# Gated linear attention and a two-layer expert on one core: all wide products in float16 halves, layer two two units behind

## The chip, the cores and the metric

The kernel runs on one core of a Trainium2 chip. The metric is the device time of one execution in microseconds. A core has TensorE (matrix products, from SBUF into PSUM), VectorE, ScalarE and GpSimd (elementwise work), and SyncE, which here issues the transfers. The engines run side by side and wait for one another by semaphores; each works through its own instructions in a fixed order.

## The reference

Two parts, one feeding the other (B=4 sequences, H=8 heads, S=768 steps, D=48 per head; 384 -> 2048 -> 384 in the expert):

```python
f = 1.0 / (1.0 + np.exp(-f_logit))
for t in range(S):
    state = f[:, :, t, :, None] * state + np.einsum('bhd,bhe->bhde', k[:, :, t], v[:, :, t])
    y[:, :, t] = np.einsum('bhd,bhde->bhe', q[:, :, t], state)
x = y.transpose(0, 2, 1, 3).reshape(B * S, H * D)
h = x @ w_in
g = np.where(h >= 1, h, np.where(h <= -1, 0.0, (h + 1) ** 2 / 4))
out = g @ w_out
```

The weights come as float64 and the result is float32.

## The kernel before

The 768 steps are cut into six blocks of 128 (NI = 6). Within a block the attention of a pair of heads is done by products of scores, values and the carried state; a block's 4 x 128 tokens (N = 512 columns) then go through the expert. The expert works in *units*: unit k is block i = k // 16 and 128 of the 2048 hidden channels, j = k % 16. Layer one of a unit is nine matmuls of 128x128 weights by 128x512 values (three thirds of the input, three terms each) into one of two PSUM banks `ph`; layer two is nine more (three thirds of the output, three terms each) that accumulate over the 16 units of a block into the three banks `po`. There are 96 units, and so 1728 of these *wide products*.

The three terms make up for the narrow operands: a value is split into a rounded part and a remainder, and the product is rounded x rounded, rounded x remainder and remainder x rounded. In blocks 0 and 1 all parts are float32r (`mm_in` L356, `mm_out` L390). From block FROM = 2 on, only the rounded x rounded term is float32r; the other two take float16 (`mm_in_16` L363, `mm_out_16` L397). For that, every weight is converted once during block 1: `convert` (L534, L535) makes float16 copies on ScalarE in a staging tile and a transfer (L537) puts them in the place of `w_lo`; each late unit also makes a float16 copy of its rounded activations (`act_16`, L377) and each attention result one of its rounded part (L862).

Between the layers a unit takes five steps: `act_1` (L366, ScalarE) and `act_2` (L369, ScalarE) make the square branch, `act_3` (L374, VectorE) the maximum and minimum, `act_hi` (L380, ScalarE) the rounded part, `act_lo` (L383, VectorE) the remainder. The weights arrive as float64 words: `split_piece` takes the bits apart (L514 ScalarE, L516 VectorE) and splits them into `w_hi` (L520, ScalarE) and `w_lo` (L521, VectorE), one piece for each unit of layer one (384 columns) and twelve pieces of layer two (512 columns), during block 0.

In blocks 0 and 1 layer two runs one unit behind: nine of layer one, nine of layer two. From block 2 on it runs by pairs of units: eighteen of layer one, eighteen of layer two. The attention of the next block is put between. `TURNS` says behind which unit a pair's keys are transposed (L840 on TensorE for block 1, L854 on VectorE after that), and `VISITS` gives four places for each two pairs: scores (`scores_of_two`, L814), states (`states_by_parts`, L1004), the begin of the output (`begin`, L892) and its end (`outputs`, L892 and L923). A place k is behind layer one of unit k, k.5 behind the layer two that follows. A visit borrows a `ph` bank and gives it back when its masks (L826) or sums (L1008) are done. `begin` ends with a small copy (L903, ScalarE) for which the next products of the visit wait. `outputs` rounds the result (L876 and L877, later L860 and L861) and issues moves (L965) that fill the remaining rows of the block's input; the first unit of the block waits for them. `largest` (L871) takes the maximum of the rounded part, which the closing test reads.

Everything is entered into a plan as an operation with an engine, a cost and its dependencies; `Plan.order` plays it through with the table COST and gives each engine its order, the operation with the least room first. `early` on an operation ranks it sooner.

Of the kernel before, what the change touches and what calls it, by code (L numbers as in the profile page):

```python
# [10 lines left out]
F32 = mybir.dt.float32  # L11
# [30 lines left out]
FROM, UP, MOST = 2, 14, 16.0  # L42
SLACK, WITHIN = 2500, 1200
# [15 lines left out]
COST = dict(mm=227, narrow=120, mm16=216, late=690, narrow16=114, scores=1000, scores_half=500, heads=940, thirds=940, half=330, both=940, begin=430, before=880, part=450, states=700, before_half=440, parts=730, parts_last=730, zeros=4860, turn=395, first=160, last=200,  # L59
# [176 lines left out]
def gla_moe(ctx: ExitStack, tc: tile.TileContext, ff, kqd, f0, vv, vad, vbd, wd, fixedd, gates, values, headsd, out):  # L236
# [14 lines left out]
    v_all = const.tile([C, 2 * B * 4 * D], F32, name="v")  # L251
    v = [v_all[:, k * B * 4 * D:(k + 1) * B * 4 * D].rearrange("u (b h e) -> u b h e", b=B, h=4) for k in range(2)]
# [9 lines left out]
    forms, x_hi = {}, tiles(2, [128, NP - 1, N], F32R, "x_hi")  # L262

    def of_form(name, shape, form):
# [5 lines left out]
    def form_of(i):  # L270
        return "late" if i >= FROM else "early"

    def x_at(i):
        return x_hi[i % 2], of_form(f"x{i % 2}", [128, NP - 1, N], form_of(i))

    def y3_at(i):
        return of_form("y3", [R, 2, N], form_of(i))

    def glo_at(k):
        return of_form(f"glo{k % 2}", [128, N], form_of(k // NJ))  # L280

# [9 lines left out]
    w_16 = w_lo.rearrange("p n c -> p (n c)").bitcast(F16).rearrange("p (n k t c) -> p n k t c", n=2 * NW, t=2, c=128)  # L291
# [5 lines left out]
    later = const.tile([128, 2 * B * D], F32, name="later")[:R]  # L297
    ds.append(const.tile([128, 2 * B * D], F32, name="ds")[:R])
# [39 lines left out]
    def w_in_16(t, j, kt):  # L338

        return w_16[:, j // 4 * 3 + kt, j % 4, t]  # L340

    def w_out_16(t, j, e):
        n, c = divmod(j * DM + e * 128, W)
        return w_16[:, NW + n, c // 128, t]

    def of_16(t):

        return t.bitcast(F16)[..., 0:N], t.bitcast(F16)[..., N:]

# [4 lines left out]
    def mm_in(ps, xt, j, c=ALL, to=ALL, a=0, z=9):  # L354
        for n, (kt, high, t) in list(enumerate(TERMS_IN))[a:z]:
            nc.tensor.matmul(ps[:, to], w_in(w_hi if high else w_lo, j, kt), xt[t][:, kt, c], start=(n == 0), stop=(n == 8))  # L356

    def mm_in_16(ps, xt, j, which):
        for n in which:
            for kt in range(3):  # L360
                low, x_16 = of_16(xt[1][:, kt])
                a, b = ((w_in_16(0, j, kt), x_16), (w_in_16(1, j, kt), low), (w_in(w_hi, j, kt), xt[0][:, kt]))[n]
                nc.tensor.matmul(ps, a, b, start=(n == 0 and kt == 0), stop=(n == 2 and kt == 2))  # L363
# [21 lines left out]
    def mm_out(hi, lo, j, es, terms, c=ALL, of=ALL):  # L385
        for e in es:
            for n in terms:
                part, g = ((w_hi, hi), (w_lo, hi), (w_hi, lo))[n]

                nc.tensor.matmul(po[e][:, c], w_out(part, j, e), g[:, of], start=(j == 0 and n == 0 and c.start == 0), stop=(j == NJ - 1 and n == 2))  # L390

    def mm_out_16(hi, lo, j, es, terms):
        low, g_16 = of_16(lo)
        for e in es:
            for n in terms:
                a, b = ((w_out(w_hi, j, e), hi), (w_out_16(0, j, e), g_16), (w_out_16(1, j, e), low))[n]
                nc.tensor.matmul(po[e], a, b, start=(j == 0 and n == 0), stop=(j == NJ - 1 and n == 2))  # L397
# [13 lines left out]
    def copy_out(e, o, up=0):  # L411
        (by_scalar if e == 1 else by_vector)(o, po[e], up)
# [34 lines left out]
    set_ds = add("POOL", 200, lambda: fresh(ds[0][:, 2 * B * D:]))  # L447
# [45 lines left out]
    def split_piece(k):  # L493
# [31 lines left out]
    last_use, again_of = {}, {}  # L525

    passing = []

    def convert(key, n, hi, lo, to):

        m = len(passing)
        past = passing[m - 6:m - 5]
        mem = raw[2 + m % 6 // 2].bitcast(F16)[:, m % 2 * 2 * W:m % 2 * 2 * W + 2 * n].rearrange("p (k t c) -> p k t c", t=2, c=128)
        o = sca(COST["copy"] * n // W, lambda: nc.scalar.activation(mem[:, :, 0], lo.bitcast(F32), AF.Copy, scale=2.0 ** UP), split[key], past, piece[-3:])  # L534
        z = sca(COST["copy"] * n // W, lambda: nc.scalar.copy(mem[:, :, 1], hi.bitcast(F32)), o)  # L535
        z.slack = SLACK
        passing.append(add("SP", "near", lambda: nc.sync.dma_start(to.bitcast(F32), mem.bitcast(F32)), z, last_use[key], kb=n // 2))  # L537
        passing[-1].slack = SLACK
        again_of[key] = passing[-1:]

    def convert_unit(j):

        at = (slice(None), slice(j // 4 * 3, j // 4 * 3 + 3), slice(j % 4 * 128, j % 4 * 128 + 128))
        convert(("unit", j), 384, w_hi[at], w_lo[at], w_16[:, j // 4 * 3:j // 4 * 3 + 3, j % 4])

    def convert_piece(c):

        convert(c, W, w_hi[:, c].rearrange("p (k c) -> p k c", c=128), w_lo[:, c].rearrange("p (k c) -> p k c", c=128), w_16[:, c])
# [6 lines left out]
    def small_piece(c):  # L555

        cuts = 2 if c < 9 else 1
        mem = raw[2 + c % 3]
        loaded = [dma(mem[:, k:k + W // cuts], wd[c, :, k:k + W // cuts], 8 * 128 * W / 1024 / cuts, seen[-6:-4] or passing[-6:])
# [8 lines left out]
    def split_again(c):  # L568
# [17 lines left out]
        nc.scalar.copy(w_hi[:, c], val)  # L586
        nc.vector.tensor_tensor(out=w_lo[:, c], in0=val, in1=w_hi[:, c].bitcast(F32), op=ALU.subtract)
# [91 lines left out]
    def elementwise(n):  # L679
# [14 lines left out]
        if p == NP - 1:  # L694

            cols = slice(0, 2 * N + B) if i else slice(0, N)
            gone = old(n - NP, "sc", "y", "tr", "db")
            c["to"] = []
            for t, m in enumerate(ours):
                o = gates_of[m]  # L700
                d = [o["km"], o["qm"], o["pf"][0]] if i else o["km"]
                o["to"] = [move(kq[NP - 1][z + 16 * SLICE[t]:z + 16 * SLICE[t] + 16, cols], kq[t][r:r + 16, cols], 64 if i else 32, d, set_kq, gone) for r, z in ((48, 0), (112, 64))]
                c["to"].extend(o["to"])
        c["kq"] = c["to"] if p == NP - 1 else [gates_of[m][a] for m in ours for a in ("km", "qm")]
        c["db"] = []
        if i > 0:
# [7 lines left out]
            c["db"].append(sca(B * COST["decay"], decayed, d, state_of[i - 1, p // 2], old(n - 4, "y", "se"), set_ds))  # L714
# [143 lines left out]
    def rounded_16(b, yf, to, y, past, cost=None):  # L858
        hi, low, x_16 = (lambda n=n: to()[n] for n in range(3))
        eh = sca(cost or "round", lambda: nc.scalar.activation(hi(), yf, AF.Copy, scale=2.0 ** UP), y, past)  # L860
        el = vec(cost or "dve", lambda: nc.vector.scalar_tensor_tensor(out=low(), in0=yf, scalar=2.0 ** UP, in1=hi().bitcast(F32), op0=ALU.mult, op1=ALU.subtract), eh)  # L861
        es = sca(cost or "copy", lambda: nc.scalar.activation(x_16(), hi().bitcast(F32), AF.Copy, scale=2.0 ** -UP), eh)  # L862
        banks[b] = [eh, el]
        return [eh, el, es]

    seen_x = {}

    def largest(i, t, *deps):

        at = 1 + NG + 6 * NW + NT * (i - FROM) + t  # L870
# [34 lines left out]
    def outputs(n, unit, alone, joint=False):  # L905
# [36 lines left out]
        def third(t):  # L942
            return [moved.get(i - 1)] if t == NT else [free]
# [567 lines left out]
```

## Time and profile before

| | |
|---|---|
| median of 3 runs | 458.86 us (458.3 to 459.25) |
| profiled execution | 458.67 us |
| its span, first to last instruction | 456.9 us |
| granted TensorE clock, mean | 0.999 |

The profile is of one execution. Busy time is the union of an engine's instructions; PE is TensorE's matmuls, PEld its weight loads, DVE VectorE, ACT ScalarE, POOL GpSimd, SP SyncE. Matmuls overlap in the array: one of 128x512 is shown some 0.38 us long, while the next one starts some 0.22 us after it. So the pace is read from starts, or from a run of many.

### The profile page before, as it was taken

The page shows a single profiled execution, that of the slowest core. Times are in us where ns is not written, and L with a number is a line of the kernel's source. Part 1 is how long each engine was busy: PE and PEld are TensorE (multiplying, and loading weights), DVE is VectorE, ACT ScalarE, POOL GpSimd, SP SyncE. Part 2 cuts the span into 40 slices and gives each one's busy share as a digit, 9 for nine tenths or more (in the row PEclk, how much of TensorE's full clock was granted, in tenths as well). Part 3 has the DMA queues.
Part 4 walks back from the last instruction along what each step waited for, and adds up shares of the span by engine and source line. Part 5 has one row for each costly group of instructions (what it writes and reads, how often), then busy time and mean ns, then how long its engine had stood idle before and what let it go on. Part 6 is the DMA issues. An engine that isn't in the chain of part 4 may idle for free.

```text
span 456.9 us, 11340 instructions
## 1 busy us (share of the span) xinstructions
PE 450.6 (99%) x4540; PEld 305.7 (67%) x4540; DVE 372.7 (82%) x727; ACT 330.8 (72%) x645; POOL 22.1 (5%) x67
## 2 busy tenths in 40 slices
PE   8999999999999999999999999999999999999996
PEld 4888888888888886665665656656655665556563
DVE  7988998989979989988788888966767978877423
ACT  4599999898889986676766766866656674756653
POOL 4200100010000100000100000001000000000000
PEclk9999999999999999999999999999999999999999
DMA  8897767445245356630320330320201534853001
GB/s 288 330 313 237 226 199 228 153 133 177 99 116 187 121 149 216 188 128 2 114 72 3 104 130 0 103 60 2 82 0 55 179 116 152 282 202 93 1 0 72
DMA packets 30263, 60.67 MB, mean 133 GB/s; under 512 B 4352, under 2 KB 11136, under 8 KB 30208
## 3 DMA queue, kind: packets, MB, share of 16 engines
q1 hardware_dynamic: 30208, 59.93, 40.8%
q8 instruction: 36, 0.59, 0.5%
q14 instruction: 19, 0.16, 0.1%
HBM read 44.76 MB, written 4.72 MB: 108 GB/s over the span
## 4 chain that ended last, share of the span: by engine, by line
PE 93%; DVE 3%; ACT 2%; DMA 1%; issue 1%; SPq 0%
PE ph L363 28%; PE po L397 28%; PE po L390 13%; PE ph L356 13%; PE pa L892 2%; PE pa L923 2%; PE ph L814 1%; PE pa L1004 1%; DVE f L651 1%; DVE w L644 1%; PE pa L840 1%; PE ph L1076 0%; DMA f<-in_f 0%; DVE kq L656 0%; PE pa L1046 0%
## 5 line engine op out<-in xcount | busy, mean ns | idle before, releaser
L366 ACT ACTIVATE act<-ph,half 128x512 f32<-128x512 f32 x96 | 66.0, 687 | 85.1 <-PE ph L363 62.7
L374 DVE SCALAR_TENSOR_TENSOR act<-ph,act 128x512 f32<-128x512 f32 x96 | 63.6, 687 | 49.5 <-ACT act L369 48.9
L397 PE MATMUL po<-glo_late,w_lo 128*128 128x512 f16 x382 | 88.4, 380 | 0.0
L363 PE MATMUL ph<-x_late,w_lo 128*128 128x512 f16 x384 | 88.2, 379 | 0.0
L854 DVE STREAM_TRANSPOSE kn<-kq 32x128 f32<-32x128 f32 x224 | 67.8, 303 | 3.4
L380 ACT CAST ghi<-act 128x512 fp32r<-128x512 f32 x96 | 58.5, 617 | 12.3 <-DVE act L374 11.5
L363 PEld LDWEIGHTS <-w_lo 128*128 128x128 f16 x384 | 37.0, 98 | 44.3 <-issue 0.5
L397 PEld LDWEIGHTS <-w_lo 128*128 128x128 f16 x382 | 34.7, 98 | 45.3 <-issue 8.1
L369 ACT ACTIVATE act<-act 128x512 f32<-128x512 f32 x96 | 57.2, 625 | 1.1
L363 PE MATMUL ph<-x_hi,w_hi 128*128 128x512 f32 x192 | 55.5, 424 | 0.0
L383 DVE TENSOR_TENSOR glo_late<-act,ghi 128x512 f16<-128x512 f32 x64 | 43.8, 689 | 14.0 <-PE po L397 11.1
L397 PE MATMUL po<-ghi,w_hi 128*128 128x512 f32 x192 | 49.1, 391 | 0.0
L363 PEld LDWEIGHTS ph<-x_hi,w_hi 128*128 128x128 f32 x192 | 36.2, 188 | 10.1
L397 PEld LDWEIGHTS po<-ghi,w_hi 128*128 128x128 f32 x192 | 36.1, 188 | 8.0
L377 ACT ACTIVATE glo_late<-act 128x512 f16<-128x512 f32 x64 | 38.2, 626 | 0.7 <-PE po L397 0.6
L390 PE MATMUL po<-ghi,w_hi 128*128 128x512 f32 x96 | 28.5, 398 | 0.0
L390 PE MATMUL po<-ghi,w_lo 128*128 128x512 f32 x96 | 27.7, 390 | 0.0
L390 PE MATMUL po<-glo_early,w_hi 128*128 128x512 f32 x96 | 27.7, 389 | 0.0
L356 PE MATMUL ph<-x_hi,w_hi 128*128 128x512 f32 x93 | 26.5, 393 | 0.0
L356 PE MATMUL ph<-x_early,w_hi 128*128 128x512 f32 x93 | 26.1, 389 | 0.0
L356 PE MATMUL ph<-x_hi,w_lo 128*128 128x512 f32 x93 | 26.1, 389 | 0.0
L383 DVE TENSOR_TENSOR glo_early<-act,ghi 128x512 fp32r<-128x512 f32 x32 | 22.0, 686 | 3.8 <-ACT ghi L380 3.4
(155 smaller groups left out, 651.9 us busy)
## 6 DMA issues: line engine op xcount, KB each, us to landing
kq<-in_kq SPq DMA_DIRECT2D x18, 512.0 KB, 5.0
raw_late<-in_w SPq DMA_DIRECT2D x10, 512.0 KB, 3.9
out_y<-raw SPq DMA_DIRECT2D x17, 256.0 KB, 2.2
f<-in_f SPq DMA_DIRECT2D x16, 256.5 KB, 3.3
v<-in_v SPq DMA_DIRECT2D x10, 384.0 KB, 5.1
raw<-in_w SPq DMA_DIRECT2D x7, 511.6 KB, 4.6
raw<-in_w SPq DMA_DIRECT2D x9, 383.6 KB, 4.0
raw_late<-in_w SPq DMA_DIRECT2D x12, 256.0 KB, 3.8
```

The lines of the kernel that those rows point to most:

```text
L356: nc.tensor.matmul(ps[:, to], w_in(w_hi if high else w_lo, j, kt), xt[t][:, kt, c], start=(n == 0), stop=(n == 8))
L363: nc.tensor.matmul(ps, a, b, start=(n == 0 and kt == 0), stop=(n == 2 and kt == 2))
L366: nc.scalar.activation(a, ps, AF.Relu, bias=half, scale=0.5 * 2.0 ** -up)
L369: nc.scalar.activation(a, a, AF.Square, scale=2.0 ** (up // 2))
L374: nc.vector.scalar_tensor_tensor(out=a, in0=ps, scalar=2.0 ** up, in1=a, op0=ALU.max, op1=ALU.min)
L377: nc.scalar.activation(g_16, a, AF.Copy, scale=2.0 ** -UP)
L380: nc.scalar.copy(hi, a)
L383: nc.vector.tensor_tensor(out=lo, in0=a, in1=hi.bitcast(F32), op=ALU.subtract)
L390: nc.tensor.matmul(po[e][:, c], w_out(part, j, e), g[:, of], start=(j == 0 and n == 0 and c.start == 0), stop=(j == NJ - 1 and n == 2))
L397: nc.tensor.matmul(po[e], a, b, start=(j == 0 and n == 0), stop=(j == NJ - 1 and n == 2))
L854: nc.vector.transpose(kn[n % 2][u:u + 32, ::-1, r:r + 32], src[:, :, u:u + 32])
L892: nc.tensor.matmul(held[h][1][64 * e:64 * e + D, m, T * (1 - k):][:, :T], v[pr // 2][half, b, pr % 2 * 2 + h], masked(n)[h][half, block], ...
```

## The change

All wide products take float16 operands, rounded part and remainder, in all six blocks. The scales are powers of two: weights times 2^16, attention results times 2^14, activations times 2^8, and the output is scaled back by 2^-24. `w_hi` and `w_lo` share one tile; the splits of weights, of attention results and of activations write float16 directly. `mm_in_16`, `mm_out_16`, `act_16`, `rounded_16`, `convert` and the transfers of converted weights go away, as do the pairs of units: one loop runs layer one of unit u and layer two of unit u - 2 (BEHIND_BY) in all blocks, with three tiles for the activations (HOMES_G). Inputs of blocks have four homes. Six moves take the place of twelve, each with both parts. The three output copies of a block are all on ScalarE. The maximum is also taken of blocks 0 and 1. The products of `attended` and `decayed` load 64 stationary columns instead of 48 (the tiles get 16 columns of zeros behind them), so that the rows between two heads are written too. The small copy in `begin` is ranked 2500 ns sooner, the moves of the last pair's keys get 1500 ns of slack in the plan, and all places in TURNS and VISITS are new.

```diff
-FROM, UP, MOST = 2, 14, 16.0
-SLACK, WITHIN = 2500, 1200
+UP_W, UP_X, UP_G, MOST = 16, 14, 8, 1.0
+UP, UP_Y = UP_W + UP_X, UP_W + UP_G
+BY_SCALAR = (0, 1, 2)
+BEHIND_BY, HOMES_G = 2, 3
+SLACK, WITHIN, AMONG = 2500, 1200, 1500
...
-SOONER = 2000
+SOONER, PROMPT = 2000, 2500
...
-TURNS = {4: 7.0, 6: 10.0, 8: 21.0, 10: 25.5, 12: 30.5, 14: 40.0, 16: 45.5, 18: 50.5, 20: 58.5, 22: 71.0}
-VISITS = {4: (8.0, 8.0, 11.0, 11.0), 6: (11.0, 12.5, 12.5, 12.5), 8: (22.0, 22.0, 23.5, 23.5), 10: (23.5, 28.0, 28.0, 28.0), 12: (35.5, 35.5, 36.5, 36.5), 14: (36.5, 41.0, 41.0, 41.0), 16: (49.5, 49.5, 51.5, 51.5), 18: (51.5, 56.5, 56.5, 56.5), 20: (65.0, 65.0, 74.0, 74.0), 22: (74.0, 74.0, 75.0, 75.0)}
+TURNS = {4: 5.5, 6: 10.5, 8: 19.5, 10: 25.5, 12: 34.0, 14: 39.0, 16: 47.5, 18: 55.0, 20: 59.5, 22: 69.5}
+VISITS = {4: (7.0, 7.0, 11.0, 11.0), 6: (11.0, 13.0, 13.0, 13.0), 8: (21.0, 21.0, 24.5, 24.5), 10: (24.5, 29.5, 29.5, 29.5), 12: (36.0, 37.0, 38.0, 38.0), 14: (37.0, 41.5, 41.5, 41.5), 16: (48.0, 48.0, 53.5, 53.5), 18: (53.5, 56.0, 56.0, 56.0), 20: (68.0, 68.0, 74.0, 74.0), 22: (74.0, 74.0, 75.0, 75.0)}
...
-    w_hi = const.tile([128, 2 * NW, W], F32R, name="w_hi")
-    w_lo = const.tile([128, 2 * NW, W], F32R, name="w_lo")
...
+    w_all = of_form("w_hi", W_ALL).rearrange("p n c -> p (n c)").bitcast(F16).rearrange("p (e n c) -> p e n c", e=2, n=2 * NW)
+    w_hi, w_lo = w_all[:, 0], w_all[:, 1]
...
-    def act_16(a, g_16):
-        nc.scalar.activation(g_16, a, AF.Copy, scale=2.0 ** -UP)
-
     def act_hi(a, hi):
-        nc.scalar.copy(hi, a)
+        nc.scalar.activation(hi, a, AF.Copy, scale=2.0 ** (UP_G - UP))
 
     def act_lo(a, hi, lo):
-        nc.vector.tensor_tensor(out=lo, in0=a, in1=hi.bitcast(F32), op=ALU.subtract)
+        nc.vector.scalar_tensor_tensor(out=lo, in0=a, scalar=2.0 ** (UP_G - UP), in1=hi, op0=ALU.mult, op1=ALU.subtract)
...
     def copy_out(e, o, up=0):
-        (by_scalar if e == 1 else by_vector)(o, po[e], up)
+        (by_scalar if e in BY_SCALAR else by_vector)(o, po[e], up)
...
-        h = sca("copy", lambda: nc.scalar.copy(hi, whole_val), v)
-        l = vec(COST["dve"] * n // W, lambda: nc.vector.tensor_tensor(out=lo, in0=whole_val, in1=hi.bitcast(F32), op=ALU.subtract), h)
+        h = sca("copy", lambda: nc.scalar.activation(hi, whole_val, AF.Copy, scale=2.0 ** UP_W), v)
+        l = vec(COST["dve"] * n // W, lambda: nc.vector.scalar_tensor_tensor(out=lo, in0=whole_val, scalar=2.0 ** UP_W, in1=hi, op0=ALU.mult, op1=ALU.subtract), h)
...
-    def convert(key, n, hi, lo, to):
...
-        passing.append(add("SP", "near", lambda: nc.sync.dma_start(to.bitcast(F32), mem.bitcast(F32)), z, last_use[key], kb=n // 2))
...
-        eh = sca(cost or "round", lambda: nc.scalar.copy(hi(), yf), y, past)
-        el = vec(cost or "dve", lambda: nc.vector.tensor_tensor(out=lo(), in0=yf, in1=hi().bitcast(F32), op=ALU.subtract), eh)
+        eh = sca(cost or "round", lambda: nc.scalar.activation(hi(), yf, AF.Copy, scale=2.0 ** UP_X), y, past)
+        el = vec(cost or "dve", lambda: nc.vector.scalar_tensor_tensor(out=lo(), in0=yf, scalar=2.0 ** UP_X, in1=hi(), op0=ALU.mult, op1=ALU.subtract), eh)
...
-                    nc.tensor.matmul(held[h][1][64 * e:64 * e + D, m, T * (1 - k):][:, :T], v[pr // 2][half, b, pr % 2 * 2 + h],
+                    a = (b * 4 + pr % 2 * 2 + h) * D
+                    nc.tensor.matmul(held[h][1][64 * e:64 * e + 64, m, T * (1 - k):][:, :T], v_of[pr // 2][half, a:a + 64],
...
+        c["yb"].early = PROMPT
...
-            moved[i] = [add("SP", "near", lambda t=t, r=r, z=z, n=n: nc.sync.dma_start(x_at(i)[n][r:r + 16, t].bitcast(F32), y3_at(i)[z + 16 * SLICE[t]:z + 16 * SLICE[t] + 16, n].bitcast(F32)),
+            moved[i] = [add("SP", "near", lambda t=t, r=r, z=z: nc.sync.dma_start(xs_of[i if i < 4 else i - 4][r:r + 16, t], y3s[i % 2][z + 16 * SLICE[t]:z + 16 * SLICE[t] + 16]),
                             x_of[i, NT], x_of[i, t], kb=32)
-                        for t in range(NT) for r, z in ((48, 0), (112, 64)) for n in range(2)]
-            for t in range(NT if i >= FROM else 0):
+                        for t in range(NT) for r, z in ((48, 0), (112, 64))]
+            for t in range(NT):
                 largest(i, t, x_of[i, t], moved[i])
...
-    for u in range(first_16):
+    for u in range(NI * NJ):
         unit_1(u)
         attend(u)
-        if u >= 1:
-            unit_2(u - 1)
-            converted(u - 1)
+        if u >= BEHIND_BY:
+            unit_2(u - BEHIND_BY)
         attend(u + 0.5)
-    for u in range(first_16, NI * NJ, 2):
-        units_1(u, u + 1)
...
-    for u in (NI * NJ - 4, NI * NJ - 2):
-        units_2(u)
+    for u in range(NI * NJ - BEHIND_BY, NI * NJ):
+        unit_2(u)
```

## Rows read from the trace of the kernel before

**Rows 1.** The page's table of engines: busy us (share of the span) xinstructions.
```profile
PE 450.6 (99%) x4540; PEld 305.7 (67%) x4540; DVE 372.7 (82%) x727; ACT 330.8 (72%) x645; POOL 22.1 (5%) x67
```

**Rows 2.** Chain of work in order of time, early and late: start us, us, what.
```profile
99.26 2.04 PE ph L356 x9
...
238.89 3.97 PE po L397 x18
```

**Rows 3.** TensorE in order of time, one late unit pair: start us, us, group xcount.
```profile
204.18 1.52 PE L397 MATMUL po<-ghi,w_hi 128*128 128x512 f32 x6
205.55 2.76 PE L397 MATMUL po<-glo_late,w_lo 128*128 128x512 f16 x12
```

**Rows 4.** Groups of weight loads by line: busy us, mean ns | idle before.
```profile
L397 PEld LDWEIGHTS po<-ghi,w_hi 128*128 128x128 f32 x192 | 36.1, 188 | 8.0
L397 PEld LDWEIGHTS <-w_lo 128*128 128x128 f16 x382 | 34.7, 98 | 45.3 <-issue 8.1
```

**Rows 5.** Chain of work in order of time, around three visits.
```profile
74.91 0.59 PE pa L892 x32
75.51 0.04 PE ph L814
...
76.44 0.89 PE pa L923 x64
77.33 0.45 PE pa L892 x32
...
86.79 2.27 PE ph L356 x9
...
198.97 1.40 PE po L397 x6
```

**Rows 6.** Waits of 133 to 138 us (total us, times, longest), and the chain there.
```profile
PEld pa L923 <- ACT seen_y L903: 0.8, 1, 0.8
...
135.38 0.62 ACT ghi L380
135.99 0.07 ACT seen_y L903
...
136.10 1.11 PE pa L923 x64
```

**Rows 7.** Busy us of four stretches: length, engines (xcount), granted clock, DMA share, GB/s.
```profile
22.60:72.00 49.40, 49.40 (x412) 41.03 (x411) 45.84 (x79) 47.66 (x95) 3.78 (x9) 1.00 0.75 245
72.00:92.00 20.00, 20.00 (x447) 16.82 (x446) 17.40 (x32) 18.13 (x38) 0.00 (x0) 1.00 0.56 175
92.00:175.00 83.00, 82.39 (x841) 67.55 (x840) 75.16 (x160) 72.70 (x151) 4.29 (x15) 1.00 0.46 141
175.00:420.00 245.00, 245.00 (x2479) 147.89 (x2478) 201.52 (x392) 162.03 (x312) 7.02 (x21) 1.00 0.33 104
```

**Rows 8.** ScalarE's first conversion in time; groups that leave, move or are added.
```profile
92.27 0.51 ACT L534 ACTIVATE raw<-w_lo 128x384 f16<-128x384 f32 x1
...
L377 ACT ACTIVATE glo_late<-act 128x512 f16<-128x512 f32 x64 | 38.2, 626 | 0.7 <-PE po L397 0.6
...
L871 DVE TENSOR_REDUCE ok<-x_hi 128x1 f32<-128x512 f32 x12 | 7.8, 676 | 0.0
L407 DVE TENSOR_SCALAR raw<-po 128x512 f32<-128x512 f32 x7 | 4.8, 679 | 1.5 <-PE po L397 1.5
```

**Rows 9.** SyncE: the last move of block 1, and issues by line with us to landing.
```profile
95.66 0.59 SPq L965 DMA_DIRECT2D x_early<-y_early  x1
...
x_early<-y_early SPq DMA_DIRECT2D x6, 32.0 KB, 1.9
```

**Rows 10.** Chain of work in order of time, the end.
```profile
452.37 0.45 PE po L1121 x4
```

**Rows 11.** ScalarE, VectorE and TensorE in order of time, around unit 8.
```profile
56.48 0.51 ACT L520 CAST w_hi<-bits 128x384 fp32r<-128x384 f32 x1
57.24 0.55 DVE L521 TENSOR_TENSOR w_lo<-bits,w_hi 128x384 fp32r<-128x384 f32 x1
57.60 0.84 PE L356 MATMUL ph<-x_hi,w_hi 128*128 128x512 f32 x3
```

More of the change, by code (lines that the diff above doesn't have):

```diff
@@ L58 @@
 LATENCY = dict(PE=235, ACT=140, DVE=110, POOL=150)
-COST = dict(mm=227, narrow=120, mm16=216, late=690, narrow16=114, scores=1000, scores_half=500, heads=940, thirds=940, half=330, both=940, begin=430, before=880, part=450, states=700, before_half=440, parts=730, parts_last=730, zeros=4860, turn=395, first=160, last=200,
+COST = dict(mm=216, narrow=114, scores=1000, scores_half=500, heads=940, thirds=940, half=330, both=940, begin=430, before=880, part=450, states=700, before_half=440, parts=730, parts_last=730, zeros=4860, turn=395, first=160, last=200,
             rows=316, turned_rows=150, scan=1140, dve=602, small=200, sums=467, gate=600, act=575, bits=660, round=485, copy=520, turned=412, sig=538, decay=226,
@@ L352, in gla_moe, with mm_in @@
     ALL = slice(0, N)
-    def mm_in(ps, xt, j, c=ALL, to=ALL, a=0, z=9):
+    def mm_in(ps, xt, j, c=ALL, to=ALL, a=0, z=9, ws=None):
         for n, (kt, high, t) in list(enumerate(TERMS_IN))[a:z]:
[L356 to L363, printed above, removed]
+            nc.tensor.matmul(ps[:, to], w_in((ws or (w_hi, w_lo))[1 - high], j, kt), xt[t][:, kt, c], start=(n == 0), stop=(n == 8))
     def act_1(ps, a, up=0):
@@ L446, in gla_moe @@
     set_rec = add("POOL", 800, lambda: fresh(rec))
-    set_ds = add("POOL", 200, lambda: fresh(ds[0][:, 2 * B * D:]))
+    set_ds = [add("POOL", 200, lambda a=a: fresh(a)) for a in (ds[0][:, 2 * B * D:], ds[1][:, 2 * B * D:], later[:, 2 * B * D:], v_all[:, 2 * BD + 16:])]
     def constants():
@@ L585, in split_again @@
             nc.vector.tensor_tensor(out=val, in0=val, in1=sign, op=ALU.mult)
-        nc.scalar.copy(w_hi[:, c], val)
-        nc.vector.tensor_tensor(out=w_lo[:, c], in0=val, in1=w_hi[:, c].bitcast(F32), op=ALU.subtract)
+        nc.scalar.copy(ws[0][:, c], val)
+        nc.vector.tensor_tensor(out=ws[1][:, c], in0=val, in1=ws[0][:, c].bitcast(F32), op=ALU.subtract)
     banks = {k: [] for k in range(8)}
@@ L702, in elementwise @@
                 o["to"] = [move(kq[NP - 1][z + 16 * SLICE[t]:z + 16 * SLICE[t] + 16, cols], kq[t][r:r + 16, cols], 64 if i else 32, d, set_kq, gone) for r, z in ((48, 0), (112, 64))]
+                for l in o["to"]:
+                    l.slack = AMONG if i else 0
                 c["to"].extend(o["to"])
@@ L856, in transpose_rows @@
         c["tr"] = c["kn"][-1]
[L858 to L864, printed above, removed]
     seen_x = {}
     def largest(i, t, *deps):
-        at = 1 + NG + 6 * NW + NT * (i - FROM) + t
+        at = 1 + NG + 6 * NW + NT * i + t
         seen_x.setdefault(i, []).append(vec("dve", lambda: nc.vector.tensor_reduce(
-            out=ok[:, at:at + 1], in_=x_hi[i % 2][:, t].bitcast(F32), axis=mybir.AxisListType.X, op=ALU.max, apply_absolute_value=True), *deps))
+            out=ok[:, at:at + 1], in_=x_at(i)[0][:, t], axis=mybir.AxisListType.X, op=ALU.max, apply_absolute_value=True), *deps))
     def rounded(b, yf, to, y, past, cost=None):
         hi, lo = (lambda n=n: to()[n] for n in range(2))
-        eh = sca(cost or "round", lambda: nc.scalar.copy(hi(), yf), y, past)
-        el = vec(cost or "dve", lambda: nc.vector.tensor_tensor(out=lo(), in0=yf, in1=hi().bitcast(F32), op=ALU.subtract), eh)
+        eh = sca(cost or "round", lambda: nc.scalar.activation(hi(), yf, AF.Copy, scale=2.0 ** UP_X), y, past)
+        el = vec(cost or "dve", lambda: nc.vector.scalar_tensor_tensor(out=lo(), in0=yf, scalar=2.0 ** UP_X, in1=hi(), op0=ALU.mult, op1=ALU.subtract), eh)
         banks[b] = [eh, el]
@@ L947, in to @@
             def to(t=t):
-                hi, lo = (y3_at(i)[:, n] if t == NT else x_at(i)[n][:, t] for n in range(2))
-                return [a[:R] for a in ([hi, lo] if i < FROM else [hi, *of_16(lo)])]
-            rounding = rounded if i < FROM else rounded_16
+                return [(y3_at(i)[n] if t == NT else x_at(i)[n][:, t])[:R] for n in range(2)]
             if not alone:
                 b, ps, _ = held[h]
-                x_of[i, t] = rounding(b, wide(ps)[:R], to, y, third(t))
+                x_of[i, t] = rounded(b, wide(ps)[:R], to, y, third(t))
                 continue
@@ L958, in outputs @@
                 cols = slice(T * k, T * k + T)
-                x_of[i, t].append(rounding(b, ps[:R, :, cols], lambda to=to, cols=cols: [a.rearrange("r (b c) -> r b c", b=B)[:, :, cols] for a in to()], y, third(t), "half"))
+                x_of[i, t].append(rounded(b, ps[:R, :, cols], lambda to=to, cols=cols: [a.rearrange("r (b c) -> r b c", b=B)[:, :, cols] for a in to()], y, third(t), "half"))
             by.append(x_of[i, t][0][:2])
@@ L1012, in states_by_parts @@
         if i < NI - 1:
-            z = vec("sums", lambda: nc.vector.tensor_tensor(out=s, in0=sums[1], in1=later, op=ALU.add), c["st"], o)
+            z = vec("sums", lambda: nc.vector.tensor_tensor(out=s, in0=sums[1], in1=later[:, 0:2 * B * D], op=ALU.add), c["st"], o)
             state_of[i, p // 2] = [z]
@@ L1114, in last_of_all @@
         t = outs[len(put) % 3]
+        hi, lo = ghi[unit % HOMES_G], glo[unit % HOMES_G]
         for n, (engine, copy) in enumerate(((vec, by_vector), (sca, by_scalar))):
             cs = cols_of(n)
-            def some(n=n, cs=cs):
-                low, g_16 = of_16(glo_at(unit))
-                for k, b in enumerate((g_16, low)):
-                    nc.tensor.matmul(po[2][:, cs], w_out_16(k, NJ - 1, 2), b[:, cs], start=False, stop=n == 1 and k == 1)
-            o = add("PE", 2 * COST["narrow16"], some, *need, many=2)
-            o = engine("small", lambda cs=cs, copy=copy: copy(t[:, cs], po[2][:, cs], UP), o, put[-3])
+            o = add("PE", 2 * COST["narrow"], lambda cs=cs: mm_out(hi, lo, NJ - 1, (2,), (1, 2), cs), *need, many=2)
+            o = engine("small", lambda cs=cs, copy=copy: copy(t[:, cs], po[2][:, cs], UP_Y), o, put[-3])
             dma(out[NI - 1, :, 2, cs], t[:, cs], 128, o)
         closing.append(o)
-    outs = [raw[0].bitcast(F32)[:, 0:N], raw[0].bitcast(F32)[:, N:2 * N], raw[1].bitcast(F32)[:, 0:N]]
+    outs = [spare[:, (6 + k) * N:(7 + k) * N] for k in range(3)]
     put = []
@@ L1261, in gla_moe @@
         work[kind](*n)
+    for t in range(NT):
+        largest(0, t, x_of[0, t])
     for k in range(len(order)):
@@ L1374, in gla_moe @@
     with tc.If(fits < 1, label="general"):
-        x0 = x_hi[0], of_form("x0", [128, NP - 1, N], "general")
-        glo = [of_form(f"glo{k}", [128, N], "general") for k in range(2)]
+        x0 = [of_form(f"x{k}", X_ALL, "general") for k in range(2)]
+        g_hi, g_lo = (of_form(f"g{k}", [128, N], "general") for k in range(2))
+        ws = [of_form(name, W_ALL, "general") for name in ("w_hi", "w_lo")]
         for c in range(2 * NW):
-            split_again(c)
+            split_again(c, ws)
         heads = const.tile([R, 2], F32, name="heads")
@@ L1424, in gla_moe @@
                 act_3(s, a)
[L1425 to L1427 removed]
+                nc.scalar.copy(hi, a)
+                nc.vector.tensor_tensor(out=lo, in0=a, in1=hi.bitcast(F32), op=ALU.subtract)
+                mm_out(hi, lo, j, range(3), (0, 1, 2), ws=ws)
             for e in range(3):
[L1429 to L1430 removed]
+                copy_out(e, act[e % 2])
+                nc.sync.dma_start(out[bass.ds(i, 1), :, e].rearrange("o r n -> (o r) n"), act[e % 2])
 def kernel(q, k, v, f_logit, moe_w_in, moe_w_out):
```

208 lines of the change are left out of this document (54 added, 154 removed).

## The prediction

> **What bounds the kernel now.** I read the table of engines first, then the chain of work that ended last, then single stretches. TensorE is busy 99% of the span [rows 1], and that figure alone proves nothing, since the ends of matmuls are modelled. The chain in order of time settles it: stretch after stretch is nothing but wide products, nine in 2.04 us in the early blocks and eighteen in 3.97 us in the late ones [rows 2], one starting when the array can take it. From 22.6 us on almost nothing makes TensorE wait, and its granted clock is full in the four stretches that I cut from 22.6 to 420 us [rows 7]. So the time is the number of products times their pace, plus the attention work between them, plus a start of 22.6 us and a tail. There are 96 units of 18 products, 1728 in all, before and after. What matters is their pace.
>
> The second thing to see is how full the engines behind TensorE are. From 22.6 to 72 us ScalarE is busy 47.7 of 49.4 us and VectorE 45.8; from 92 to 175 us 72.7 and 75.2 of 83; after 175 us ScalarE falls to 66% and VectorE to 82% [rows 7]. In the first stretch the kernel has two bounds that nearly coincide.
>
> **The pace of the products.** Early products are all float32r: 2.04 / 9 = 227 ns each [rows 2]. In a late block the order is readable: six float32r products from 204.18 to 205.55 us, 1.37 us or 228 ns each, then twelve float16 ones whose starts lie (2.76 - 0.38) / 11 = 216 ns apart, the last one's 0.38 us taken off [rows 3]. The change makes all 1728 float16, both operands. A unit then takes 18 x 216 = 3.89 us.
> - Blocks 0 and 1: 32 units now take 2 x 2.04 = 4.08 us; 32 x 0.19 = 6.1 us less.
> - Blocks 2 to 5: 64 units now take 3.97 us; 64 x 0.082 = 5.3 us less.
> That is 11.4 us, on the bound itself, with nothing hiding it.
>
> The weight loads show the same split: 98 ns for a float16 128x128 load, 188 ns for a float32r one [rows 4]. The Trainium skill says otherwise ("TensorE: Matmul & The Clock Gate", section "LDWEIGHTS (loading the stationary operand)"): a load takes its columns divided by 1.2 GHz whatever is in them, 107 ns for 128 columns as an estimate from that page. By that rule the type would change nothing in the loads; the trace disagrees, and I keep the trace. What the rule would give if pace followed it is a rival below.
>
> **Entering the products after attention.** Where float32r products follow small ones in the early blocks, the first nine take 2.27 us in the chain instead of 2.04; where float16 ones follow in block 2, six take 1.40 instead of 1.30 (six times 216 ns): 0.23 against 0.10 [rows 5]. The early blocks have eleven such entries, seven behind small products and four behind transposes, which no float16 product follows in this trace; I count those four half: 9 x 0.13 = 1.1 us less. Bounds: nothing to 1.4 us (all eleven).
>
> **The one real stall.** At 134 to 136 us the chain leaves TensorE: it runs through a unit's steps on ScalarE and VectorE, then the 0.07 us copy at L903, which stood in ScalarE's queue behind L380, and only then come the products of L923 [rows 6]. TensorE misses 0.61 us in that stretch (82.39 of 83 us [rows 7]) and its weight loads wait 0.8. The change ranks that copy 2.5 us earlier (PROMPT). I book 0.8 us; bounds 0 and 0.8. The cost is that ScalarE may stand waiting for TensorE in front of a unit's copies; there it has idle time.
>
> **Wider small products.** The second half of attention (L892, L923) loads 64 stationary columns instead of 48, 1280 products in all. The trace has both widths with equal moving columns: 64 score products with 64 columns take 0.93 us (75.51 to 76.44), 64 with 48 columns take 0.89 [rows 5]. 1280 / 64 x 0.04 = 0.8 us more; bounds 0 and 1.6 (twice that).
>
> **The placing.** Visit 12 gets a place of its own for its states (36, 37, 38 where it was 35.5, 36.5): one interruption more. An interruption costs its entry, 0.10, and the slower first group of small products, 0.59 against 0.45 [rows 5]: 0.25 us. Bounds 0 and 0.5.
>
> **What costs nothing.** Sixty-four copies to float16 (626 ns each) and 56 conversions of weights leave ScalarE; the first conversion starts at 92.27 us and the copies lie after 175 [rows 8]. With the conversions go 28 transfers to w_lo (16 units and 12 pieces) and their SyncE issues. Eleven output copies of some 0.68 us move from VectorE to ScalarE, and six maxima of 676 ns are added on VectorE [rows 8]. All that is off the chain, under TensorE's products; if VectorE fell behind there it would cost up to the 4 us of the maxima, but the planner can put these anywhere. Six moves instead of twelve fill a block's rows: the last was issued at 95.66 and landed some 2 us later [rows 9], 1.5 us before unit 16 starts at 99.1; issuing six saves 6 x 0.63 = 3.8 us of that queue, which the one block less between the visit and the unit needs. Three more memsets on GpSimd cost it some 0.3 us in front of its first copy. The last four narrow products stay, so I leave the tail as it is [rows 10].
>
> **Where the change asks for more than there is.** No relief falls before 92 us, and there TensorE asks sooner. Layer two now follows two units behind, so each unit's weights are wanted one 2.04 us block earlier; visit 4 moves from 8.0 to 7.0, and its products (0.93 us of scores, about as long for the states) now stand before unit 8. Unit 8 would start at 57.6 - 2.04 - 14 x 9 x 0.011 + 1.8 = 56.0 us instead of 57.60. Its rounded weights were ready at 56.48 + 0.51 = 57.0, 0.6 us ahead, and VectorE's remainder at 57.79, 1.2 ahead of the third group of products [rows 11]. So some 1.0 us is missing. Against it: the layer-two piece split just before unit 8 is wanted later now. For it: ScalarE idles only 1.7 of 49.4 us up to 72 us [rows 7], a visit's masks come sooner, and both engines work in a fixed order, in which one late step holds all behind it. I take 1.5 us of new waits before 72 us; bounds 0 and 5.8 (rival 1).
>
> **The sum.** From the profiled execution's 458.67 us (span 456.9 and 1.8 around it): -11.4 - 1.1 - 0.8 + 0.8 + 0.25 + 1.5 = 447.9. The median of the runs, 458.86, is 0.2 above the profiled one, so 448.1 us.
>
> **The rivals.**
> 1. *The first stretch is bound by ScalarE.* It has 47.7 us of work in 49.4 and the change takes none of it away there. Then units 0 to 15 keep their time (16 x 0.19 = 3.1 us of pace and 0.9 of entries are lost) and the earlier visit waits its own 1.8 us: 5.8 instead of 1.5, or 452.4 us, spread over 450.5 to 455. For it: the 0.6 us of slack at unit 8. Against it: the spare room in VectorE and the layer-two pieces that may wait.
> 2. *Each visit stalls.* In place of pairs of units with 18 products on end, every unit is now nine and nine, so a visit has half the cover for its ScalarE copy and VectorE masks. If each of 16 visits waits like the one at 136 us, 0.8 us each, that is 12.8 us: 448.1 + 12.8 = 460.9, slower than before. It decides from 11 / 16 = 0.7 us per visit, one step of a unit in the queue. Against it: the early visits already run between nines and only one of them stalled.
> 3. *The pace does not depend on the type.* If the float16 products owed their 216 ns to their place in the block, 11.4 and 1.1 us would go: 460.6. The rows of a late block speak against it, as float32r gives 228 ns right beside 216. This is what the skill's column rule would do here.
>
> **Chances.** Forecast, 445.2 to 450.5: 0.72. Rival 1: 0.20. Rival 2: 0.06. Rival 3: 0.02. The low end takes the kind bounds together: no early waits (-1.5), no cost of the 64 columns (-0.8) or of the extra interruption (-0.25), entries at 1.4 (-0.3), 445.2. The range goes up to 453.0, past the middle of rival 1, and leaves out the rest of it and rivals 2 and 3, some 0.16. A change of 0.2% is about what a measurement of this kernel can tell from none. Faster by more: 0.92, all of the forecast and of rival 1; within: 0.02; slower: 0.06, most of rivals 2 and 3.
>
> **What would show it.** In the trace after, nine wide products should take 1.94 us in the chain everywhere, every load of 128 columns 98 ns, and the conversions be gone. Waits of TensorE before 72 us show the early term: a unit's first product waiting for ScalarE's or VectorE's split. If these sum to 4 us or more, rival 1 holds; waits of 0.7 us at L923 or at the unit after most visits mean rival 2; nines of 2.04 us rival 3. The prediction is also wrong if the granted clock falls below full in stretches where it is full now.

## The result and the profile after

The changed kernel takes 447.6 us (median of 6 runs, 446.9 to 448.37) against 459.04 us (458.3 to 459.32) before: a ratio of 0.9753, 95% interval 0.9741 to 0.9766. Forecast were 448.1 us, 445.2 to 453.0. The profiled execution took 447.77 us, its span is 446.0, its granted clock 1.000.

The page of the kernel after: its table of engines (busy us, share of the span, instructions), the shares of the chain that ended last, and two groups of weight loads (busy us, mean ns | idle before); it answers to [rows 1, 4]:

```profile
PE 439.2 (98%) x4540; PEld 223.3 (50%) x4540; DVE 371.4 (83%) x724; ACT 271.3 (61%) x519; POOL 27.7 (6%) x70
...
PE 81%; DVE 7%; DMA 5%; ACT 3%; SPq 2%; issue 1%; DVEq 0%
...
L372 PEld LDWEIGHTS <-w_hi_usual 128*128 128x128 f16 x866 | 83.8, 98 | 99.6
L348 PEld LDWEIGHTS <-w_hi_usual 128*128 128x128 f16 x855 | 83.2, 98 | 99.8 <-issue 0.9
```

All loads of the wide products take 98 ns, where float32r loads took 188 [rows 4], and ScalarE has 59.5 us less to do. The chain of work in order of time (start us, us, what) shows the pace; it answers to [rows 2, 5]:

```profile
74.54 2.05 PE po L372 x9
76.58 1.94 PE ph L348 x9
...
98.87 1.94 PE ph L348 x9
...
134.39 0.47 PE pa L837 x32
134.85 2.05 PE ph L348 x9
...
239.41 2.05 PE po L372 x9
241.46 1.94 PE ph L348 x9
```

Nine products take 1.94 us early and late, where they took 2.04 early and half of 3.97 late. The first nine behind small products take 2.05: an entry of 0.11 us, where float32r paid 0.23. Busy us by stretch (length; PE, PEld, DVE, ACT, POOL; granted clock; DMA share; GB/s) answer to [rows 7]:

```profile
22.60:72.00 49.40, 49.16 (x505) 26.08 (x505) 47.41 (x82) 46.08 (x93) 5.86 (x9) 1.00 0.78 251
72.00:92.00 20.00, 19.42 (x380) 10.96 (x371) 19.69 (x35) 18.95 (x43) 0.95 (x3) 1.00 0.81 267
92.00:175.00 83.00, 82.84 (x860) 41.03 (x859) 76.48 (x159) 51.54 (x104) 7.95 (x15) 1.00 0.32 93
175.00:420.00 245.00, 245.00 (x2498) 121.53 (x2497) 200.66 (x398) 132.91 (x246) 5.94 (x18) 1.00 0.26 82
```

The clock is full in all four. TensorE now misses a little in the first three, where before it missed only in the third. I also cut TensorE's whole time by the kind of product, counting from each matmul's start to the next one's start, so that a wait counts with the product ahead of it:

| us | before | after | change | booked |
|---|---|---|---|---|
| until the first wide product | 22.59 | 22.71 | +0.12 | 0 |
| wide products | 387.90 | 375.37 | -12.53 | -12.4 (pace -11.4, entries -1.1, one entry more +0.1) |
| all others, with the waits behind them | 42.03 | 43.40 | +1.37 | +1.65 (-0.8 + 0.8 + 0.15 + 1.5) |
| from the last product's start to the end | 4.35 | 4.50 | +0.15 | 0 |
| span | 456.9 | 446.0 | -10.9 | -10.75 |

What the table can't tell is whether each term is there for the reason that the prediction gave. The runs below ask that.

### The profile page after: what moved, and what is told of

The parts are those of the page before. It is cut to its first block, busy times and chain, and to the rows that moved or that the text cites. A ratio compares the mean times of both kernels' runs of the same rounds, so it can differ in the third digit from the quotient of the medians.

```text
span 446.0 us, 11014 instructions
## 1 busy us (share of the span) xinstructions
PE 439.2 (98%) x4540; PEld 223.3 (50%) x4540; DVE 371.4 (83%) x724; ACT 271.3 (61%) x519; POOL 27.7 (6%) x70
## 4 chain that ended last, share of the span: by engine, by line
PE 81%; DVE 7%; DMA 5%; ACT 3%; SPq 2%; issue 1%; DVEq 0%
PE po L372 37%; PE ph L348 36%; PE pa L837 2%; PE pa L869 2%; DMA raw_late<-in_w 2%; DVE bits L491 2%; PE ph L766 1%; DMA raw<-in_w 1%; ACT bits L489 1%; DVE w_hi_usual L496 1%; PE pa L948 1%; DMA act<-in_f 1%; SPq L909 1%; DVE w L594 1%; DVE g_usual L365 1%
## 5 line engine op out<-in xcount | busy, mean ns | idle before, releaser
L372 PE MATMUL po<-g_usual,w_hi_usual 128*128 128x512 f16 x866 | 202.0, 379 | 0.0
L372 PEld LDWEIGHTS <-w_hi_usual 128*128 128x128 f16 x866 | 83.8, 98 | 99.6
L348 PEld LDWEIGHTS <-w_hi_usual 128*128 128x128 f16 x855 | 83.2, 98 | 99.8 <-issue 0.9
L348 PE MATMUL ph<-x_usual,w_hi_usual 128*128 128x512 f16 x567 | 132.7, 379 | 0.0
L362 ACT ACTIVATE g_usual<-act 128x512 f16<-128x512 f32 x96 | 60.2, 627 | 45.2 <-DVE act L359 45.0
L365 DVE SCALAR_TENSOR_TENSOR g_usual<-act,g_usual 128x512 f16<-128x512 f32 x96 | 65.9, 687 | 13.4 <-ACT g_usual L362 10.7
L348 PE MATMUL ph<-w_lo_usual,w_hi_usual 128*128 128x512 f16 x288 | 67.5, 379 | 0.2 <-DMA w_lo_usual<-y 0.2
L594 DVE TENSOR_TENSOR_SCAN w<-f,least_w 128x512 f32<-128x512 f32 (+1 forms) x18 | 20.7, 1157 | 1.9 <-ACT f L590 1.8
L601 DVE TENSOR_TENSOR_SCAN f<-f,rec 128x512 f32<-128x512 f32 (+1 forms) x18 | 20.8, 1158 | 0.1
L514 DVE TENSOR_REDUCE ok<-raw 128x1 f32<-128x512 f32 x30 | 19.5, 678 | 0.0
L496 DVE SCALAR_TENSOR_TENSOR w_hi_usual<-bits,w_hi_usual 128x384 f16<-128x384 f32 (+1 forms) x28 | 16.8, 603 | 0.3 <-ACT w_hi_usual L495 0.3
L837 PEld LDWEIGHTS pa<-am,v 64*64 64x64 f32 x608 | 11.3, 134 | 4.5 <-issue 2.5
L604 DVE TENSOR_TENSOR kq<-kq,w 128x512 f32<-128x512 f32 (+1 forms) x20 | 12.4, 620 | 0.1
L489 ACT ACTIVATE bits<-raw,top_of 128x384 uint32<-128x384 fp8e4 (+1 forms) x16 | 10.9, 698 | 2.0 <-DMA raw<-in_w 2.0
```

Of the source, the lines that this page charges most:

```text
L348: nc.tensor.matmul(ps[:, to], w_in((ws or (w_hi, w_lo))[1 - high], j, kt), xt[t][:, kt, c], start=(n == 0), stop=(n == 8))
L362: nc.scalar.activation(hi, a, AF.Copy, scale=2.0 ** (UP_G - UP))
L365: nc.vector.scalar_tensor_tensor(out=lo, in0=a, scalar=2.0 ** (UP_G - UP), in1=hi, op0=ALU.mult, op1=ALU.subtract)
L372: nc.tensor.matmul(po[e][:, c], w_out((ws or (w_hi, w_lo))[part], j, e), g[:, c], start=(j == 0 and n == 0 and c.start == 0), stop=(j == N ...
L496: l = vec(COST["dve"] * n // W, lambda: nc.vector.scalar_tensor_tensor(out=lo, in0=whole_val, scalar=2.0 ** UP_W, in1=hi, op0=ALU.mult, op ...
L594: s1 = vec(COST["scan"] if count == 1 else 602, lambda bwd=bwd, u0=u0, u1=u1: nc.vector.tensor_tensor_scan(out=wide(w[:, u0:u1]), data0=bw ...
```

## The experiments

Times are medians; each is set beside the kernel before in the same session (458.92 to 459.07 us).

**Does the type set the pace?** Two kernels differ in one thing, the type of two fixed tiles that the rounded-by-rounded term of blocks 1 to 5 reads in place of its own operands. The rest of the computation is kept.

```diff
+    w_32, x_32 = const.tile([128, 128], F32R, name="w_32"), const.tile([128, N], F32R, name="x_32")
...
+            if fixed_32 and high and t == 0:
+                nc.tensor.matmul(ps[:, to], w_32, x_32[:, c], start=(n == 0), stop=(n == 8))
+                continue
```

> The kernel after, but in the 80 units of blocks 1 to 5 the six products of rounded weight by rounded value (three in layer one, three in layer two) read one fixed float32r weight tile and one fixed float32r value tile, so that term is not the reference's and the rest is as it was; the order of the work and the plan's costs are unchanged. Theory (the pace goes with the type of the operands): six of 18 products take 227 to 228 ns instead of 216, as in the late blocks of the kernel before, 6 x 0.012 to 0.014 = 0.07 to 0.086 us a unit, 5.8 to 6.9 us in all: 453.4 to 455.1 us, with nines of 1.98 us in the chain and loads of 188 ns in these places. Rival (the pace goes with the place of a product in its unit or with the block): 447.6 to 448.2 us, nines stay at 1.94 us.

> The same kernel with the two fixed tiles in float16 instead of float32r: the term is left out in the same way and only the type differs from the run beside it. Both theories: as the kernel after, 447.6 to 448.2 us, nines of 1.94 us. If this one too is slower, it is the fixed tiles (no new operand to wait for, one address read again and again) and not the type that the other run shows.

Measured: 461.23 us (460.96 to 461.74) with float32r, 450.14 us (449.83 to 450.31) with float16. The float16 control missed its 447.6 to 448.2: the copies that fill the tiles stand at the start, and the first wide product starts at 23.7 us in both kernels instead of 22.7, which is 1.0 of some 2 us; most of the rest lies between the small products, which with their waits take 44.6 us against 43.4. Its nines are 1.94 us, so the fixed tiles do not change the pace, and the two are compared with each other alone: 11.1 us for the type. The chain of the float32r kernel, eighteen products in a late block:

```profile
300.06 1.31 PE po L379 x6
301.37 0.69 PE ph L350 x3
302.06 1.31 PE ph L352 x6
303.38 0.69 PE po L376 x3
```

The chain of the float16 kernel:

```profile
295.12 0.65 PE ph L350 x3
295.77 1.29 PE ph L352 x6
297.07 0.65 PE po L376 x3
```

And the float32r kernel's weight loads by line and shape (busy us, mean ns | idle before):

```profile
L352 PEld LDWEIGHTS <-w_hi_usual 128*128 128x128 f16 x615 | 53.6, 98 | 75.0 <-issue 22.3
L350 PEld LDWEIGHTS ph<-x,w 128*128 128x128 f32 x240 | 45.1, 189 | 14.7
```

The same products at the same places in the same order take 2.00 us a nine with three float32r among them and 1.94 without. The rival that the pace goes with the place is out. The size was missed, 11.1 against 5.8 to 6.9. Three products at the 227 ns of [rows 2] would take 0.68, and with six of 216 ns that is 1.98, where two nines here take 4.01 (300.06 to 304.07): some 0.03 us of each nine is for going from one type to the other and back. This kernel does that four times in 36 products, a late block of before once (its two eighteens of 3.97 hold 12 x 0.227 + 24 x 0.216 = 7.91 us, so 0.03 in 36). The rest lies at the entries. Behind small products the first three take 0.90 us in the float32r kernel and 0.75 in the float16 one, and only 0.03 of that difference is the pace:

```profile
187.47 0.90 PE po L376 x3
```

```profile
184.94 0.75 PE po L376 x3
```

Of the 160 nines 13 are entered like that. An estimate from these rows, 480 x 0.011 for the pace, 147 x 0.03 for the changes of type and 13 x 0.12 for the entries, is 11.3 us; 11.1 were measured.

**Do the 64 columns cost 0.8 us?** The kernel before with this part of the change alone (`a:a + 64` for `a:a + D` in `attended` and `decayed`, and zeros behind the tiles).

> The kernel before with 64 stationary columns in the 1280 products of attended and decayed, and nothing else. Theory: 64 products take 0.93 us in place of 0.89, 0.8 us more in all. Rival (loads are hidden): no difference beyond 0.2 us.

Measured: 459.92 us, ratio 1.0022 (1.001 to 1.0034), so +1.0 us (0.5 to 1.6). Its chain, the visit at 136 us of [rows 6]:

```profile
135.97 0.93 PE pa L926 x64
136.91 0.47 PE pa L895 x32
```

They are 0.89 and 0.45 with 48 columns [rows 5]. This kernel's stall at 136 us is gone as well, though the edit was not aimed at it, so the +1.0 of the whole is not the price of the columns alone. Counted from start to start, the 1280 products themselves take 20.31 us where they took 19.39: +0.9, and the price holds. The stall was worth some 0.8 the other way, and other small differences of the order make up the rest.

**What does the earlier rank of the small copy (PROMPT) do?** Taken away from the kernel after, and given alone to the kernel before.

```diff
-        c["yb"].early = PROMPT
```

> The changed kernel without the earlier rank of the small copy in begin. Theory (the copy's place in ScalarE's queue decides): waits of L869 on that copy come back, 0.8 us each at one or two visits, so 0.8 to 1.6 us slower than the changed kernel. Rival (new places alone removed the wait at 136 us): within 0.2 us of it.

> The kernel before with that one rank added and nothing else. Theory: the wait of 0.6 to 0.8 us near 136 us goes and the time falls by 0.8 us. Rival: ScalarE then stands waiting for TensorE in front of a unit's copies, and the time stays within 0.2 us or rises.

Measured without it: 449.13 us, ratio 0.978 (0.9758 to 0.9802); the kernel after in the same session, below, has 0.9771 (0.975 to 0.9792). By their times they can't be told apart; by their waits the theory fails, as in both TensorE waits for this copy once, at 72 to 73 us, and nowhere else. Measured with it alone in the kernel before: 464.06 us, ratio 1.0114 (1.0092 to 1.0136): 5.1 us slower where 0.8 faster was expected. The profiled execution is the fastest of the six, 462.29, and shows 3.6 us of it in its span (460.5 against 456.9); where the others lose the rest is not shown (the granted clock of four of them is 0.994 to 0.996, 0.998 here). Its chain and its waits of TensorE (us in total, times, longest):

```profile
133.83 0.59 PE pa L892 x32
134.42 1.19 PE po L461 x5
...
136.70 0.89 PE pa L924 x64
```

```profile
PE ph L814 <- DVE act L374: 1.9, 1, 1.9
```

The stall at 136 us is gone, and in its place stand five products of zeros (L461), with which the plan fills time in which it foresees TensorE idle; and at 197 us the scores wait 1.9 us for VectorE, which they did not before. One rank of one copy of 0.07 us changed the order of much that stands behind it. The theory that this copy's rank is worth 0.8 us fell.

> The changed kernel again, as the mark for the others of this group. Both theories: 447.6 us, and in the trace every group of nine wide products 1.94 us, the waits of TensorE as in the first profile (at the visit near 71 us, and 0.3 us at 165 us).

The kernel after again: 448.18 us (447.93 to 448.64). The same program waits some 0.3 us more in this execution, at unit 8, which here waits for VectorE.

**What does the second unit of distance buy?** `BEHIND_BY = 1` in the kernel after.

> The changed kernel with layer two one unit behind in place of two, all places as they are. Theory: the last unit's steps of some 4 us have only nine products of cover, so the end gets some 2 us later, and block 0 waits 0 to 2 us more for late steps: 2 to 4 us slower than the changed kernel. Rival (the lag only moves the demand for weights one block sooner): waits before 72 us go and the kernel is 0.5 to 1 us faster.

Measured: 451.0 us, ratio 0.9826 (0.9805 to 0.9848). Against the two ratios of the kernel after, 0.9753 and 0.9771, that is 2.5 to 3.4 us more than with two. Part of it is the end, where layer two of the last unit has only zeros to stand behind, in the chain:

```profile
441.66 1.29 PE po L436 x6
442.96 2.01 PE po L372 x11
```

**How near is rival 1?** The rounded activations are written twice, in 16 units of block 0 or of block 3: 16 more copies on ScalarE.

```diff
+        if 0 <= k < 16:
+            o = g["hi"] = sca("copy", lambda: act_hi(a, hi), o)
```

> The changed kernel with each unit's rounding on ScalarE done twice in units 0 to 15, some 0.53 us of ScalarE each, 8.5 us in all. Theory (ScalarE has 3.3 us of idle time up to 72 us and 1 up to 92): TensorE loses 4 to 8 us. Rival (ScalarE is full only because the plan has it work ahead): within 1 us of the changed kernel.

> The same doubling in units 48 to 63 (block 3), where ScalarE is busy some 55% of the time. Theory: nothing, within 0.3 us of the changed kernel. Rival (the longer chain of a unit's steps costs, wherever it is): as much as in block 0.

Measured: 454.15 us (453.59 to 454.24), ratio 0.9887 (0.9867 to 0.9906), in block 0, 5.3 to 6.2 us more than the kernel after; 447.86 us (447.73 to 448.32), ratio 0.9756 (0.9737 to 0.9775), in block 3, nothing. Their stretches, first the kernel with more work in block 0, then the one with more in block 3:

```profile
22.60:72.00 49.40, 48.99 (x495) 25.83 (x494) 46.84 (x80) 48.92 (x101) 5.88 (x9) 1.00 0.76 242
```

```profile
175.00:420.00 245.00, 245.00 (x2499) 121.59 (x2497) 201.00 (x397) 142.89 (x262) 5.26 (x18) 1.00 0.26 82
```

The size in block 0 is the theory's 4 to 8 us, but the theory said that TensorE would lose it where ScalarE is full, and it does not. ScalarE is busy 48.92 of 49.40 us there, and its work falls behind (unit 14's rounding starts at 94.39 us instead of 91.85); yet the same nine of TensorE at the end of block 0, with 14 of the 16 copies done, starts 0.67 us sooner than in the kernel after. TensorE in order of time, first the kernel after, then the kernel with more work in block 0:

```profile
92.88 2.10 PE L372 MATMUL po<-g_usual,w_hi_usual 128*128 128x512 f16 x9
```

```profile
92.21 2.11 PE L372 MATMUL po<-g_usual,w_hi_usual 128*128 128x512 f16 x9
94.15 0.81 PE L436 MATMUL po<-zeros 128*128 128x512 bf16 x3
```

The time is lost behind that: three zeros at 94 us, fifteen in front of block 2's states, and a wait in front of unit 32 for which the profile names no cause, in the chain:

```profile
118.10 3.34 PE po L436 x15
...
161.30 1.49 issue
162.79 2.12 PE ph L348 x9
```

The zeros stand where the plan foresees TensorE idle; whether it would have waited there without them no run shows. Up to the end of block 0 the rival's price fits, within 1 us.

In the late blocks 10 us more of ScalarE's time (142.89 against 132.91) cost nothing, so the 64 copies that the change takes away from there were probably worth nothing either. The weights' conversions lay before 175 us, where no run puts work back; TensorE missed 0.61 us in all from 92 to 175 us [rows 7], at the stall.

**Do the new places matter?** `TURNS` and `VISITS` of before in the kernel after.

> The changed kernel with the places of the kernel before in TURNS and VISITS. Theory (the pace makes the gain, the places keep waits small): 0.5 to 3 us slower than the changed kernel, through waits in block 0. Rival (the new places are what carries the gain): 5 us or more slower.

Measured: 450.5 us (449.92 to 451.14), ratio 0.9812 (0.979 to 0.9833): 1.9 to 2.7 us more: so much the new places are worth in this kernel.

**Can the waits that are left be had?** Two tries on the kernel after: one with ranks (and visit 10's end half a unit sooner), one with places alone (`VISITS`: 11.5 for 11.0, 29.0 for 29.5).

```diff
-SOONER, PROMPT = 2000, 2500
+SOONER, PROMPT = 2000, 8000
...
+        if n > 3:
+            c["kn"][0].early = 4000
```

> The kernel after with the copy that the second half of attention waits for ranked 8 us early instead of 2.5, the normalised keys' copy of ScalarE ranked 4 us early from the second visits on, and place 10's visit ending at 29.0 instead of 29.5, so that block 2's moves leave half a unit sooner. Theory (the four waits of 0.3 to 0.8 us that are left at 70, 72 and 165 us are each of one step that stands late in a queue): they go, up to 1.5 us: 446.1 to 447.4 us. Rival (a rank changes the whole order of the plan, as in the run where the kernel before got the rank alone): waits of the same size come elsewhere, 447.6 to 450 us.

Measured: 448.54 us (447.94 to 449.36), no gain. The wait at 165 us is gone, the ones at 70 and 72 us stand as before: ScalarE's list from 65 to 73 us is the same, line for line, as that of the kernel after (below), although the copy is ranked 5.5 us sooner.

> The kernel after with three places moved by half a unit: visit 4's end and visit 6's scores at 11.5 instead of 11.0 (later, for the waits at 70 and 72 us) and visit 10's end at 29.0 instead of 29.5 (sooner, for unit 32's wait at 165 us), no ranks changed. Theory (these waits go): 0.3 to 1 us less, 446.6 to 447.4 us. Rival: as in the run with the old places, the plan makes up for a wait with zeros or another wait: 447.6 to 449 us.

Measured: 450.54 us (450.25 to 451.33), ratio 0.9822 (0.9806 to 0.9839), 2.3 to 3.2 us more than the kernel after. The wait at 70 us went; new ones came at units' first products, and six zeros:

```profile
118.50 1.40 PE po L436 x6
```

No version here beats the kernel after.

## Why the prediction was right, and where it was not

**The pace.** Right in mechanism and size. Nines are 1.94 us throughout, the loads 98 ns, and one term set back to float32r costs 11.1 us. Wide products gave back 12.53 us with two new waits in it, 0.33 at unit 32 and 0.3 at 70 us; 12.4 were booked. The late term was right for a reason that the prediction didn't see in full: of its 0.082 us a unit, 6 x 0.011 = 0.066 is the type and 0.016 the change between types.

The rule that the prediction quoted against this (the Trainium skill, "TensorE: Matmul & The Clock Gate", section "LDWEIGHTS (loading the stationary operand)") reckons a load by its columns alone, without a word on their type; 98 and 189 ns for the same 128 columns, side by side, disagree. The section behind it, "Weight-path perf modes — Fast Weight Load (FWL) and DoubleRow", has the exception that I passed over: a fast load is on for 128 weights of a type other than FP32, measured at about twice the speed. The trace agrees with that ratio, if float32r is counted with FP32, which the page doesn't say.

**The entries.** Right: 0.11 us for float16 behind small products, 0.23 for float32r.

**The stall at 136 us.** It went, as booked, but the step that named its cause failed: it does not come back when the copy's rank is taken away, and in the kernel before it goes with the rank alone (with five zeros in its place) and also with the 64 columns alone. So the rank was not needed; several edits that change the plan's order remove it, and which of them did it in the kernel after is not shown.

**The early waits.** 1.5 us were booked before 72 us; TensorE waits some 0.3 us at 70 us and 0.7 at 72. The size was near, the place was wrong. Unit 8 starts at 55.94 us, where the prediction's sum gave 56.0, and waits for nothing in this execution (some 0.3 us in the other). The waits are within the visit. TensorE's weight loads from 69 to 74 us (total us, times, longest), then the chain there:

```profile
PEld pa L837 <- ACT kn L795: 0.7, 1, 0.7
PEld pa L869 <- ACT seen_y L848: 0.7, 1, 0.7
```

```profile
69.25 0.54 ACT w_hi_usual L495
69.79 0.85 ACT kn L795 x2
70.65 1.24 ACT bits L489 x2
71.89 0.52 ACT g_usual L362
72.40 0.27 ACT w_hi_usual L495
72.67 0.05 issue
72.72 0.15 ACT seen_y L848
72.86 0.04 issue
72.91 1.16 PE pa L869 x64
```

ScalarE goes from one task to the next without a gap; the two copies that TensorE waits for stand behind others. It is the same kind of wait as in [rows 6], at another visit. That ScalarE is full does not explain it by itself: with 16 more copies in block 0 ScalarE has more to do, and this visit waits for neither copy; TensorE is busy 20.00 us of the 20 behind 72. So the load alone does not make the wait.

That the sum missed by only 0.5 us is partly luck: 0.8 us were booked off for a cause that the runs don't bear out, and the early waits came smaller and elsewhere, beside one that was not booked.

**Wider products.** +0.8 booked; +0.9 in the products themselves, +1.0 (0.5 to 1.6) in the time of the kernel that has them alone.

**What was not booked.** Unit 32 waits 0.33 us for block 2's moves, and about as long in the other execution. The prediction looked at block 1's only, where 1.5 us were left. In block 2 one move's issue took 1.50 us, where the others take some 0.59, in the chain:

```profile
159.55 0.51 SPq L909
...
160.74 1.50 SPq L909
...
163.54 1.95 DMA w_lo_usual<-y
...
165.63 1.67 PE ph L348 x7
```

Why that one took longer is open; the kernel before has such an issue too, 1.66 us at 227 us, where nothing waited for it. The start and the end lost 0.12 and 0.15 us, which no run took apart.

**The rivals.** Rival 1 did not come: TensorE waits 1.0 us up to 73 us, not 5.8. ScalarE does stand behind both waits, and from the start to 72.9 us the chain now runs through the other engines and the transfers; TensorE's share of it fell from 93% to 81% (84% in the other execution). But ScalarE does not set TensorE's pace in the stretch: with the added copies TensorE is no later at its end, and that kernel's 454.15 us, past the 452.4 of this rival, come from what lies behind it. Rival 2 is out: the visits behind 72 us show no such wait. So is rival 3: the type alone costs 11.1 us.

## What to carry to other kernels

Cut the bounding engine's time by kind of product and by the type of its operands: a pace read from two rows of one trace, times a count, carried this forecast, while both causes that it gave for single stalls were wrong. In a kernel whose order comes from a plan, a wait belongs to the order and not to the instruction at which it shows; of the four edits here that changed a rank or moved a place by half a unit, two cost 2 to 5 us, two nothing that the times can tell, and none gained, so book such an edit as a range and not as the wait that it is aimed at. That an engine is busy almost all the time does not make it the bound: 16 copies more on ScalarE cost nothing in block 3, where it has room, and left TensorE no later at the end of block 0, where it is full; the 5 to 6 us that they cost there came later, most of them as zeros of the plan. So look for the moment at which two kernels part before naming a cause.

## What was not expected of the hardware

Going between float32r and float16 products costs TensorE time beside what the types themselves take: some 0.03 us for each pair of changes, so that three float32r products among nine cost 0.06 us and not the 0.033 of their pace. By these numbers, grouping products by type, as the kernel before did over 36, is worth something for that alone; one that changes four times in 36 pays some 0.1 us more.
